# Attention with q and k resident in 64-key by 57-query tiles, filter rows turned on VectorE, and the FFT moved behind attention, in a fused conv and attention kernel

One core of one Trainium2 chip. The metric is device time of one execution, in microseconds, of the slowest (here: only) core. Executions of the kernel before on one chip agree within 1.6%. A run that lies more than 1.5% above the fastest of its kernel in the same comparison is labelled slow and is left out of all ratios.

## The reference

Two branches over one input `x` of 2048 rows by 640 columns, mixed by a gate:

```python
g = sigmoid((x * gate_w).sum(-1, keepdims=True))
# branch A: short conv on k (4 taps), times v, long conv by FFT (length 4096), times q (= x)
kv = shift_conv(k, shift_k) * v
y  = irfft(rfft(kv, 4096) * rfft(ssm_k, 4096))[:2048] + kv * ssm_D
a  = x * y
# branch B: 32 heads of 20, each query sees 8 keys at distances 0, 2, ..., 14
q, k, v = split(x @ wqkv)
b = softmax(q . k[pos - 2*off] * scale) v  @ wo
out = g * a + (1 - g) * b
```

All tensors are bfloat16. Even and odd rows never meet in branch B, so the rows are worked as two sequences of 1024.

## The kernel before

First, k's rows with their three predecessors are loaded for the conv; the predecessors go to 127 partitions:

```python
nc.sync.dma_start(kh[1:128, 0:3, :], raw(k2, 13 * D, [[16 * D, 127], [D, 3], [1, D]]))
```

Second, the gate is stored by rows of 128 partitions, and read back much later, in the middle of attention (POOL issues both):

```python
nc.gpsimd.dma_start(g_scr.rearrange("(c p two) -> p two c", p=128, two=2)[:, par, :], g_sb[...])
...
if s == 8:
    gate_loads()
```

Third, q and k are projected on PE, copied to a staging tile and moved by DMA, head by head, to partitions 32h: 20 rows of each head (these copies are called fragments below) and 11 rows that make the mask (called constants). They live in rings of three tiles, so most of the projection runs inside attention:

```python
dst = (qsets if which == 0 else ksets)[(h // 4) % 3]
frag = (dst[r:r + fb - fa, 0:w], stg[fa - f0:fb - f0, 0:w])
...
if 6 <= s < 36:
    advance(qk, 1)          # projection step inside attention
```

Fourth, attention works on 128 keys by 121 queries: six or eight score products of 121 columns, one exponential, and as many products with the values for each half (a half is two of the four heads of a tile, over one group of key blocks). The output projection is interleaved with the FFT. Fifth, in the last stage four products come straight off PSUM on DVE, and the table `T` is loaded only when the inverse FFT has left its memory.

The softmax here doesn't subtract the row's maximum and nothing guards it: scores larger than these inputs give would overflow.

Of the kernel before, what the change touches and what calls it, by code (L numbers as in the profile page):

```python
# [20 lines left out]
H = 32  # L21
# [4 lines left out]
BP = 121  # L26
NB = 17
PRE = 7
HS = 1024 + PRE
XW = 2072  # L30
NF = 11
NT = 8
KW = 128 * NB
QW = BP * NB
GROUPS = [[0, 1, 2, 3], [4, 5, 6, 7], [8, 9, 10], [11, 12, 13], [14, 15, 16]]
# [39 lines left out]
def attn_consts():  # L75
    B, C = 256.0, 512.0
    kk = np.arange(128); qq = np.arange(BP)
    kc = kk // 8 - 8; ko = kk % 8; qc = qq // 8 - 8; qo = qq % 8
    sk = np.where(kc % 2 == 0, 1.0, -1.0); sq = np.where(qc % 2 == 0, 1.0, -1.0)
    mk = np.zeros((NF, 128)); mq = np.zeros((NF, BP))  # L80
    mk[0] = kc * kc; mk[1] = kc; mk[2] = 1.0
    mq[0] = -B; mq[1] = B * (2 * qc + 1); mq[2] = -B * (qc * qc + qc) - C / 2
    for v in range(8):
        mk[3 + v] = sk * (ko == v)
        mq[3 + v] = (C / 2) * sq * np.where(v < qo, -1.0, 1.0)
    tot = np.einsum("fk,fq->kq", mk, mq)
    dlt = kk[:, None] - qq[None, :]
    inb = (dlt >= 0) & (dlt <= 7)
    assert (tot[inb] == 0).all() and (tot[~inb] <= -C / 2).all()
    for m in (mk, mq):  # L90
        assert (_np_bf16(m).astype(np.float64) == m).all()
    pos = BP * np.arange(NB)[None, :] - PRE + kk[:, None]
    valid = (((pos >= 0) & (pos < 1024)) | ((pos >= HS) & (pos < HS + 1024))).astype(np.float32)
    return dict(mk=_np_bf16(np.tile(mk, (1, NB))), mq=_np_bf16(np.tile(mq, (1, NB))),
                valid=_np_bf16(valid), ident=_np_bf16(np.eye(128)))


def ccol(sb):
    return PRE + 128 * sb + (PRE if sb >= 8 else 0)


def pos_rows(x2, p0, n):
    out = []
    for par in range(2):
        a, b = max(p0, HS * par), min(p0 + n, HS * par + S // 2)
        if a < b:
            v = x2.rearrange("(e two) d -> two e d", two=2)
            out.append((a - p0, b - a, v[par, a - HS * par:b - HS * par, :]))
    return out
# [31 lines left out]
def kernel(  # L141
# [31 lines left out]
    xS = p0.tile([128, 16, D], BF, name="xS", tag="A")  # L173
    vn = p0.tile([128, 16, D], BF, name="vn", tag="Hslot")
    Dz = p0.tile([128, 160], BF, name="Dz")
    F1b = p0.tile([128, 128], BF, name="F1b")
    M = p0.tile([128, 2, 128], BF, name="M")
    g_sb = p0.tile([128, 16], F32, name="g_sb")
    g_nat = p0.tile([128, 16], F32, name="g_nat")
    omg = p0.tile([128, NB], F32, name="omg")  # L180
    oTs = []
    for e in range(3):
        oTb = p0.tile([128, NDT, 128], BF, name=f"oT{e}")
        oTs.append(oTb)
# [3 lines left out]
    VWs = [p0.tile([128, NB, H // 2, 21], BF, name="VWa", tag="VWa"), pA.tile([128, NB, H // 2, 21], BF, name="VWb")]  # L188
    valid = pA.tile([128, NB], BF, name="valid")
    ksets, qsets, ETs = [], [], []  # L190
    for e in range(3):
        kb = pA.tile([128, KW], BF, name=f"kb{e}")
        qb = pA.tile([128, QW], BF, name=f"qb{e}")
        ksets.append(kb); qsets.append(qb)
    NET = 6
    for e in range(NET):
        ETb = pA.tile([128, 2, 512], BF, name=f"ET{e}")
        ETs.append(ETb)
    sB = ExitStack()
    p1 = sB.enter_context(tc.tile_pool(name="pB", bufs=1, side="right", reuse_waits="tile"))  # L200
# [4 lines left out]
    wg = pC.tile([128, NDT], BF, name="wg")  # L205
    wl = pC.tile([128, 4, D], BF, name="wl")


    W3 = B_wqkv.rearrange("(t p) (w n) -> p t w n", p=128, w=3)
    xq4 = x2.rearrange("(t p two) d -> p two t d", p=128, two=2)  # L210
    khs = [None] * 4

    def load_x(c):
        nc.sync.dma_start(xS[:, 4 * c:4 * c + 4, :], xq4[:, c // 2, 4 * (c % 2):4 * (c % 2) + 4, :])
# [4 lines left out]
    def load_kv(c):  # L219
        kh = p1.tile([128, 7, D], BF, name="kh", tag="kh", bufs=2)  # L220
        khs[c] = kh
        t0 = 4 * c
        eng = nc.sync if c < 2 else nc.gpsimd
# [3 lines left out]
        eng.dma_start(kh[:, 3:7, :], raw(k2, t0 * D, [[16 * D, 128], [D, 4], [1, D]]))  # L227
        eng.dma_start(vn[:, t0:t0 + 4, :], raw(v2, t0 * D, [[16 * D, 128], [D, 4], [1, D]]))

    nc.sync.dma_start(ident[:], ca["ident"].ap())  # L230
    for c0, c1 in ((0, PRE), (HS, HS + PRE), (2 * HS, XW)):
        nc.gpsimd.memset(xT[:, :, c0:c1], 0.0)
    load_x(0); load_w(2); load_x(1)
    wraw = p1.tile([128, D, 4], BF, name="wraw", tag="stg", bufs=2)
# [3 lines left out]
    load_kv(0)  # L238
    load_x(2); load_x(3)
    load_w(0); load_w(1)  # L240
    load_kv(1)
    nc.gpsimd.memset(Dz[:], 0.0)
    nc.gpsimd.memset(omg[:], 0.0)
    for e in range(NET):
        nc.gpsimd.memset(ETs[e][:], 0.0)
    for e in range(3):
        nc.gpsimd.memset(oTs[e][:], 0.0)
    for e in range(2):
        nc.gpsimd.tensor_copy(VWs[e][:, :, :, DH], valid[:].unsqueeze(2).to_broadcast([128, NB, H // 2]))

    def load_feats(e):
        for h4 in range(4):
            nc.sync.dma_start(ksets[e][32 * h4 + DH:32 * h4 + DH + NF, :], ca["mk"].ap())
            nc.sync.dma_start(qsets[e][32 * h4 + DH:32 * h4 + DH + NF, :], ca["mq"].ap())

    load_feats(0)
    for q in range(4):
        nc.gpsimd.dma_start(Dz[32 * q:32 * q + 1, :], A_ssm_D[160 * q:160 * q + 160].unsqueeze(0))
# [6 lines left out]
    def kv_gen():  # L265
        nc.vector.tensor_copy(wl[:], wraw[:].rearrange("p c j -> p j c"))
        pr = p0.tile([128, 4, 4 * D], BF, name="pr", tag="Kslot")
        yield
        for c in range(4):
            kh = khs[c]  # L270
            if c:
                nc.vector.tensor_copy(kh[:, 0:3, :], khs[c - 1][:, 4:7, :])
            for j in (0, 1, 3, 2):
                nc.vector.tensor_tensor(pr[:, j].rearrange("p (n c) -> p n c", n=4), kh[:, 3 - j:7 - j, :],  # L274
                                        wl[:, j, :].unsqueeze(1).to_broadcast([128, 4, D]), ALU.mult)
                yield
            nc.vector.tensor_tensor(pr[:, 0:2], pr[:, 0:2], pr[:, 2:4], ALU.add)
            yield
# [3 lines left out]
                                    vn[:, 4 * c:4 * c + 4, :].rearrange("p n (u i) -> p n u i", u=8), ALU.mult)  # L282
            nc.gpsimd.dma_start(raw(kvs, 4 * c * 80, [[16 * 80, 128], [S * 80, 8], [1, 320]]),
                                pr[:, 2].rearrange("p (u m) -> p u m", u=8))
            if c < 2:
                load_kv(c + 2)
            yield

    kvg = kv_gen()

# [4 lines left out]
    def transposes(c):  # L295
        for d0 in (0, 2, 4):
            nd = min(2, NDT - d0)
            tr = ppv.tile([128, 2, 4, 128], BF, name="trx", tag="trx")
            for dd in range(nd):
                for k in range(4):  # L300
                    nc.tensor.transpose(tr[:, dd, k, :], xS[:, 4 * c + k, 128 * (d0 + dd):128 * (d0 + dd) + 128], ident[:, :])  # L301
            ld.copy(xT[:, d0:d0 + nd, ccol(4 * c):ccol(4 * c) + 512],
                    tr[:, 0:nd].rearrange("p d k c -> p d (k c)"), 512 * nd, eng="a")

    def vproj(b):
        ps = ppv.tile([128, 1024], F32, name="psv", tag="psv")
        for n0, n1 in ((0, 512), (512, 640)):
            for dt in range(NDT):
                nc.tensor.matmul(ps[:, n0:n1], lhsT=xT[:, dt, BP * b:BP * b + 128], rhs=W[:, dt, 2, n0:n1],  # L309
                                 start=(dt == 0), stop=(dt == NDT - 1))  # L310
        for e in range(2):
            nc.scalar.copy(VWs[e][:, b, :, 0:DH], ps[:, 320 * e:320 * e + 320].rearrange("p (h d) -> p h d", h=H // 2))

    def gate():
        gps = ppv.tile([128, 16], F32, name="gps", tag="trx")
        for sb in range(16):
            for dt in range(NDT):
                nc.tensor.matmul(gps[:, sb:sb + 1], lhsT=xT[:, dt, ccol(sb):ccol(sb) + 128], rhs=wg[:, dt:dt + 1],
                                 start=(dt == 0), stop=(dt == NDT - 1))
        nc.scalar.activation(g_sb[:], gps[:], ACT.Exp, scale=-1.0)  # L320
        nc.vector.tensor_scalar(g_sb[:], g_sb[:], 1.0, None, ALU.add)
        nc.vector.reciprocal(g_sb[:], g_sb[:])
        for par in range(2):
            nc.gpsimd.dma_start(g_scr.rearrange("(c p two) -> p two c", p=128, two=2)[:, par, :],
                                g_sb[:, 8 * par:8 * par + 8])

    def gate_loads():
        gs = g_scr[:]
        nc.gpsimd.dma_start(omg[0:BP, 0:8], raw(gs, 0, [[2, BP], [2 * BP, 8]]))
        nc.gpsimd.dma_start(omg[0:56, 8:9], raw(gs, 2 * 968, [[2, 56], [1, 1]]))  # L330
        nc.gpsimd.dma_start(omg[63:BP, 8:9], raw(gs, 1, [[2, 58], [1, 1]]))
        nc.gpsimd.dma_start(omg[0:BP, 9:16], raw(gs, 2 * 58 + 1, [[2, BP], [2 * BP, 7]]))
        nc.gpsimd.dma_start(omg[0:119, 16:17], raw(gs, 2 * 905 + 1, [[2, 119], [1, 1]]))
        for g in range(4):
            nc.gpsimd.dma_start(g_nat[32 * g:32 * g + 32, :], raw(gs, 16 * g, [[64, 32], [1, 16]]))

# [378 lines left out]
```

## Time and profile before

| | before |
|---|---|
| median of 2 runs | 352.71 us (352.31 to 353.11) |
| PE, DVE, ACT busy | 72%, 60%, 47% of the span |
| attention starts, ends | 86 us, 212 us |
| FFT with output projection ends | 320 us |
| last stage | 34 us, 10 of them empty |

No engine is full, so the time is a sum of stages. The prediction shows the lines that carry this: engine use by stage, three waits, and the data rate in the front.

### The profile page before, as it was taken

The numbers are of one execution on the slowest core, as the hardware profiler recorded it, in microseconds if no ns is written. First come the engines' busy times: TensorE is split into PE (matmuls) and PEld (weight loads), VectorE is DVE, ScalarE is ACT, GpSimd is POOL, SyncE is SP. The second block draws the span as 40 slices with busy tenths as digits, with TensorE's granted clock in tenths as the row PEclk, the third lists the DMA queues.
The fourth block names the chain that finished last, engine by engine and source line by source line (L and its number), as shares of the span: only waits on it lengthen the run. The fifth ranks groups of instructions, "written<-read, shape, count | busy, mean of one in ns | idle before, by whom it ended". The sixth has DMA issues, their size and how long they took to land. (4 is left out here: it accounts for less than half of the span.)

```text
span 354.1 us, 9846 instructions
## 1 busy us (share of the span) xinstructions
PE 254.6 (72%) x4355; PEld 174.0 (49%) x4355; DVE 211.4 (60%) x295; ACT 165.9 (47%) x239; POOL 41.2 (12%) x67
## 2 busy tenths in 40 slices
PE   2760599958779999857877888898989488660430
PEld 2330355524336655545655655575657477660320
DVE  1400999692836565857776633844574668671595
ACT  3250264525526555634545585756565577531000
POOL 8910023010150000000000000112111000000000
PEclk9995599999659999755555556999999968867555
DMA  7375854974441499761891019217121507999165
GB/s 200 137 241 178 267 151 118 211 199 102 103 84 31 88 168 163 193 191 30 181 213 51 4 27 217 65 41 170 39 54 38 138 4 164 213 213 212 57 149 132
DMA packets 34603, 46.37 MB, mean 131 GB/s; under 512 B 23757, under 2 KB 28572, under 8 KB 33152
## 3 DMA queue, kind: packets, MB, share of 16 engines
q1 hardware_dynamic: 31088, 35.77, 42.9%
q0 software_dynamic: 2896, 8.66, 9.3%
q10 hardware_dynamic: 576, 1.31, 1.6%
q8 instruction: 34, 0.56, 0.7%
q14 instruction: 9, 0.07, 0.1%
HBM read 27.19 MB, written 7.87 MB: 99 GB/s over the span
## 5 line engine op out<-in xcount | busy, mean ns | idle before, releaser
L421 ACT ACTIVATE ET<-sc 128x726 bf16<-128x726 f32 (+1 forms) x80 | 67.1, 858 | 57.8 <-PE sc L418 57.2
L352 PE MATMUL pj<-xT,W 128*128 128x484 bf16 (+3 forms) x250 | 55.9, 368 | 6.2 <-ACT stg L128 4.0
L274 DVE TENSOR_TENSOR pr<-kh,wl 128x2560 bf16<-128x2560 bf16 x16 | 23.0, 1487 | 28.2 <-DMA kh<-in_A_k_dram 23.4
L485 PE MATMUL s<-Am,G 64*128 64x64 bf16 x1280 | 29.2, 206 | 13.9 <-DVE Hs L130 4.1
L352 PEld LDWEIGHTS <-W 128*128 128x128 bf16 x250 | 21.7, 102 | 29.8 <-issue 11.9
L418 PE MATMUL sc<-qb,kb 31*128 31x121 bf16 x544 | 36.0, 260 | 0.6 <-issue 0.6
L485 PEld LDWEIGHTS <-G 64*128 64x128 bf16 x1280 | 26.1, 105 | 17.9 <-issue 12.1
L435 PEld LDWEIGHTS <-ET 128*128 128x128 bf16 x544 | 22.4, 102 | 20.8 <-ACT ET L421 9.3
L618 PE MATMUL op<-wo,oT 128*128 128x128 bf16 (+1 forms) x170 | 27.3, 310 | 4.3 <-ACT oT L128 3.5
L130 DVE CAST stg<-pj 128x484 bf16<-128x484 f32 (+3 forms) x30 | 17.9, 598 | 20.8 <-PE pj L352 16.2
L130 DVE CAST Am<-s 128x512 bf16<-128x512 f32 x36 | 23.4, 686 | 11.5 <-PE s L468 9.9
L309 PE MATMUL psv<-W,xT 128*128 128x128 bf16 (+1 forms) x170 | 27.6, 327 | 2.8 <-DMA W<-in_B_wqkv_dram 2.8
L525 PE MATMUL i<-M,Hw 128*128 128x128 bf16 x160 | 25.6, 253 | 4.9 <-DVE Hw L513 2.6
L525 PE MATMUL i<-M,Hs 128*128 128x128 bf16 x160 | 26.0, 253 | 4.1 <-DVE Hs L512 4.1
L626 POOL DMA_DIRECT2D b_scr<-fin x18 | 9.6, 531 | 161.7 <-DVE fin L624 137.9
L128 ACT CAST Am<-s 128x512 bf16<-128x512 f32 x44 | 23.6, 610 | 6.7 <-PE s L468 4.6
L525 PEld LDWEIGHTS <-Hs 128*128 128x128 bf16 x160 | 22.5, 154 | 7.0 <-DVE Hs L512 4.5
L130 DVE CAST Hs<-s 128x1024 bf16<-128x1024 f32 x15 | 18.4, 1224 | 11.7 <-PE s L485 11.7
L301 PE MATMUL trx<-ident,xS 128*128 128x128 bf16 x80 | 7.9, 265 | 22.6 <-DMA xS<-in_A_q_dram 20.4
L525 PEld LDWEIGHTS <-Hw 128*128 128x128 bf16 x160 | 22.4, 155 | 3.0 <-DVE Hw L513 3.0
L128 ACT CAST Cm<-i 128x1024 bf16<-128x1024 f32 x15 | 15.2, 1012 | 15.9 <-PE i L525 15.7
L309 PEld LDWEIGHTS <-xT 128*128 128x128 bf16 x170 | 14.7, 106 | 15.4 <-issue 7.2
(73 smaller groups left out, 362.5 us busy)
## 6 DMA issues: line engine op xcount, KB each, us to landing
Hw<-Hs SPq DMA_DIRECT2D x10, 512.0 KB
xS<-in_A_q_dram SPq DMA_DIRECT2D x4, 640.0 KB
kv_scr<-pr POOLq DMA_DIRECT2D x4, 640.0 KB, 5.4
h_lin<-in_A_ssm_k_dram SPq DMA_DIRECT2D x8, 320.0 KB
kv<-kv_scr SPq DMA_DIRECT2D x4, 640.0 KB
qg<-in_A_q_dram SPq DMA_DIRECT2D x4, 640.0 KB
bl<-b_scr SPq DMA_DIRECT2D x4, 640.0 KB
W<-in_B_wqkv_dram SPq DMA_DIRECT2D x3, 800.0 KB
```

What stands on the lines that cost most here:

```text
L128: self.nc.scalar.copy(dst, src)
L130: self.nc.vector.tensor_copy(dst, src)
L274: nc.vector.tensor_tensor(pr[:, j].rearrange("p (n c) -> p n c", n=4), kh[:, 3 - j:7 - j, :], wl[:, j, :].unsqueeze(1).to_broadcast([128, ...
L309: nc.tensor.matmul(ps[:, n0:n1], lhsT=xT[:, dt, BP * b:BP * b + 128], rhs=W[:, dt, 2, n0:n1], start=(dt == 0), stop=(dt == NDT - 1))
L352: nc.tensor.matmul(ps[:, 0:n], lhsT=W[:, dt, which, 128 * ft:128 * ft + 128], rhs=rhs, start=(dt == 0), stop=(dt == NDT - 1))
L418: nc.tensor.matmul(sc[:, hh, BP * bb:BP * bb + BP], lhsT=kb[r:r + DH + NF, 128 * b:128 * b + 128], rhs=qb[r:r + DH + NF, BP * b:BP * b + B ...
L421: nc.scalar.activation(ETs[s % NET][:, :, 0:nw], sc[:, :, 0:nw], ACT.Exp, scale=SCALE)
L435: nc.tensor.matmul(O[:, sl * 21:sl * 21 + 21], lhsT=ET[:, hh, BP * bb:BP * bb + 128], rhs=VWs[t // 4][:, b, 4 * (t % 4) + 2 * hf + hh, :], ...
L485: nc.tensor.matmul(o, lhsT=st["G"][rows, j, r, :], rhs=Am[rows, 2 * j + r, :, :], start=(r == 0), stop=(r == 1), tile_position=(64 * c, 0) ...
L525: nc.tensor.matmul(o, lhsT=src[:, c, :, :, 8 * oc + il].rearrange("p q j -> p (q j)"), rhs=M[:, k, :], start=(k == 0), stop=(k == 1), skip ...
L618: nc.tensor.matmul(opf[:, n0:n1], lhsT=oT[:, ft, :], rhs=wo[:, ft, n0:n1], start=(ft == 0), stop=(ft == NDT - 1))
L626: nc.gpsimd.dma_start(dst, fin[r0:r0 + n, :])
```

## The change

Its intent: keep all of q and k in SBUF in 64 by 57 tiles, so that attention has no projection in it and four small products lie side by side in the array (`tile_position`); take the filter's rows apart with 32x32 transposes on VectorE; and let all FFT work follow attention, so that the output projection fills attention instead. Attention then runs in three thirds, of six of the 18 key blocks and 16 halves each. The diff has 936 lines; its core:

```diff
-    xS[128, 8, D]                      # x by 128 rows, 4 loads
+    xS[128, 18, D]                     # 18 overlapping tiles of 2 x 64 rows, tag K0
+    kvw[128, 27, D]                    # all of k and two rounds of v, tag K1
+    kq0 tag K0, kq1 tag K1             # resident q and k: heads 0-15, heads 16-31
...
     def kv_gen():                      # conv, 4 rounds; kq1 can only be written when it has ended
         nc.vector.tensor_tensor(pr[:, 2], pr[:, 0], ..., ALU.mult)
         nc.gpsimd.dma_start(kv_scr[...], pr[:, 2])     # as before: pr has one buffer
...
     def gate():
-        nc.gpsimd.dma_start(g_scr.rearrange(...), g_sb)          # 128 rows, loads later
+        for e in range(2):                                       # 57 rows; 4-byte pieces as before
+            for sub in range(2):
+                nc.gpsimd.dma_start(raw(gs, ..., [[2, QB], [4 * QB, n], [1, 1]]), gat[...])
+            nc.gpsimd.dma_start(...)
+        for g in range(4):
+            nc.gpsimd.dma_start(g_nat[32 * g:32 * g + 32, :], ...)   # at once
...
+    for k in range(25):                # all q/k projection before attention
+        advance(qk, 1); advance(kvg, 1)
...
+    for q in range(4): nc.sync.dma_start(kv[...], ...)           # 2.6 MB
+    nc.sync.dma_start(G[:], ...)                                 # 2 MB
+    nc.vector.transpose(hT[...], hns[g][...])                    # 20 times, inside attention
+    # attention: 48 halves of 24 + 24 small products, one 684-column exponential each,
+    # one step of the output projection of the third before in each half
...
+    run("aaaa", a=s1_gen(("h", 0), 0))
+    qg loads, T load                   # 3.6 MB, ahead of the first swap of halves
+    run("abababab", a=h_s2(0), b=s1_gen(("u", 0), 0))
...
+    for q in range(4): nc.scalar.copy(yt[...], ps[:, q, ...])    # last stage: ACT leaves PSUM
+    nc.vector.tensor_tensor(reg, yt, reg, ALU.mult)
```

## The prediction

> **What bounds the kernel now.** I read the page's slices first (engine use and granted clock over the span), then one table of engine use by stage, then the order of time inside each stage, then the DMA view of the first 42 us. No engine is full over the span (PE 72%, DVE 60%, ACT 47%), so the time is a sum of stages, each with its own limit. Columns of the table: stretch, its length, then busy us and instruction count of PE, weight load, DVE, ACT, POOL, then granted clock, DMA share, GB/s.
>
> ```profile
> 11.00:86.00 75.00, 53.93 (x412) 30.35 (x414) 43.87 (x31) 29.35 (x63) 14.67 (x20) 0.86 0.64 176
> 86.00:143.00 57.00, 51.39 (x643) 29.67 (x643) 32.91 (x66) 30.97 (x38) 6.84 (x10) 0.88 0.58 104
> 143.00:212.00 69.00, 52.90 (x1085) 39.03 (x1085) 45.23 (x84) 36.60 (x44) 0.00 (x0) 0.52 0.45 111
> 212.00:276.00 64.00, 56.58 (x927) 39.49 (x924) 35.99 (x48) 38.48 (x56) 9.55 (x18) 0.95 0.38 92
> 276.00:320.00 44.00, 30.10 (x768) 28.30 (x767) 31.12 (x39) 26.73 (x36) 0.00 (x0) 0.81 0.68 149
> 320.00:330.00 10.00, 0.06 (x16) 0.06 (x16) 0.09 (x1) 0.06 (x1) 0.00 (x0) 0.68 0.75 184
> 330.00:354.00 24.00, 7.22 (x512) 4.94 (x512) 18.60 (x30) 0.00 (x0) 0.00 (x0) 0.50 0.45 112
> ```
>
> Front (to 86), attention with 30 of the 50 q/k projection chunks (to 143), attention with the filter FFT of three groups (to 212), FFT with output projection (to 276), FFT alone (to 320), ten empty us, the last stage. The third row matters most: the clock is halved for 69 us although PE is busy for 53 of them.
>
> Two waits explain the empty places. In the front, x arrives late; the single-engine DMA below is the reason. Near the end everything stands for T.
>
> ```profile
> PEld L301 <- DMA xS<-in_A_q_dram: 20.6, 2, 15.1
> DVE pr L274 <- DMA kh<-in_A_k_dram: 23.4, 2, 23.2
> PE i L673 <- DMA T<-cf_T: 10.9, 1, 10.9
> ```
>
> Data rate in 40 slices of the stretch from 10 to 16 us:
>
> ```profile
> GB/s 401 401 410 384 393 401 375 375 350 273 239 137 102 77 51 26 26 26 26 26 26 26 26 26 26 26 26 26 26 26 51 0 51 26 26 26 26 26 26 26
> ```
>
> The rate falls from 400 to 26 GB/s: one engine works, on the load of k's first three rows (127 partitions, 476 KB). 487 KB at 26 GB/s is some 19 to 22 us,[...] kh came at 35.8, the third piece of x at 39.05.
>
> [...]
>
> **The change part by part.**
>
> *Front.* x is now gathered as 18 overlapping tiles, and 13 of them are queued ahead of the 127-partition load, which stays. Work for those 13 on PE is some 1.7 us each[...], from 11 us as before: to about 32. Before, the slow load ran 9.4 to 31.7; the x tiles ahead of it add some 125 KB on its engine, so it ends near 38, kh lands at 42, the last five x tiles at 47. PE waits from 32 to 47, and ends values and gate at 61. Then all 50 q/k chunks run at once[...].
>
> That is not what ends the front. q and k now live in two whole tiles; the second reuses the memory of k and v of the conv. Its constants are queued on SP ahead of the third block's fragments, so SP stands until DVE has done the conv: starting at 42, four rounds of 13.5 us (before: 35.8 to 76.4 for three) end at 96. Constants then take some 7 us and the fragments of that block some 10 (174 KB each; before 85 KB took 0.71 us to issue, or 120 GB/s). The staging tile is double, so the fifth block waits until 114, and its last tiles run cold. Attention begins at 121 (before: 86). Here is the price of keeping q and k resident: 35 us later, against 30 chunks (150 matmuls of some 0.2 us, 31 us) taken out of attention.
>
> *Attention.* 80 exponentials become 48. From 726 columns 778 ns and 968 columns 977 ns, one of 684 is 743 ns: ACT falls from 67.1 to 35.7 us, and it isn't the limit. PE at the halved clock before: the eight scores of one half took 0.54 us, eight values products 0.32[...].
>
> ```profile
> 204.31 0.39 PE L435 MATMUL O<-VWb,ET 128*128 128x21 bf16 x8
> 204.63 0.59 PE L418 MATMUL sc<-qb,kb 31*128 31x121 bf16 x8
> 205.48 0.39 PE L435 MATMUL O<-VWb,ET 128*128 128x21 bf16 x8 [0.27 <-ACT ET L421]
> ```
>
> After: 24 and 24 smaller matmuls for each half, four side by side. The only 16-tile stage here (last stage, 32x32 tiles) made 93 in 1.25 us, 13.4 ns for load and matmul. If issue sets that, 48 x 13.4 + 0.2 = 0.85 us[...]. I take 1.15. First third (16 halves): 18.5 us. In the others the output projection of the third before is mixed in, on average 1.2 us cold or 0.6 warm: 32 x 2.45 = 78 us cold, 32 x 1.5 = 48 warm. Before, with 5 projection matmuls of about 1.0 us in 1.55 us the clock was full; with FFT matmuls of 0.97 in 2.36 it stayed halved. The new mix is 40 to 53%, so I give cold 70%: 70 us. Then the last six projections alone: 13.[...] Attention and projection end at 121 + 18.5 + 70 + 13 = 222 (attention alone ended at 212 before).
>
> *FFT.* Now all five filter groups stand here and no projection. Vector work for a group: 16 copies of 512 columns (0.60 ACT, 0.69 DVE), 12 of 1024 (1.01, 1.23), four products of 1.22: shared out, 14 us. PE at full clock: 64 first-stage matmuls 1.8, 256 second-stage 4.4, 64 inverse 4.1, 10.3 us, and 18 at the halved. So it is vector-bound by a little when warm. With hand-overs 15.5 a group; start 17, three groups with scaling of qg 49, last 24: 90 us (before 108). End 312.
>
> *Last stage.* T is loaded early: the empty ten us go. Before, a round is four products off PSUM and one sum, 3.43 us on DVE. Now four copies on ACT (0.58 each, 2.3) beside two DVE operations of 1.16: 2.32. With 6.1 us of scaling bl (16 x 0.38) in front: about 5 + 12.6 + 4 for the last stores = 22 (before 34).
>
> Sum: 121 + 101 + 90 + 22 = 334; I say 333.
>
> **The rivals.** (1) Small tiles pay[...]. Attention is 60 us in place of 88, total some 305. For it: i2's 13.4 ns; against it: 69 us of halved clock before. (2) [...]everything stays cold: 1.5 us a half, attention 24 + 89, FFT partly cold at 105: total some 370. (3) SP isn't held up as I say, because the conv starts sooner or the last blocks overlap: attention at 105, total 317. The wait for kh of 23.2 us speaks against it. (4) Saturated DMA at the end of the front[...] runs into attention and costs 10 more.
>
> **Range and chances.** The parts are uncertain by about 15 (attention), 8 (FFT), 6 (front), 4 (rest): together 18.5, so 24 either way for 8 in 10. 2% faster is 345.7, 0.7 of that deviation away: faster 0.76, same 0.16, slower 0.08.
>
> **What would show it.** A front with a PE gap near 32 to 47 and another near 104 to 114, SP waiting for DVE's last conv product; attention starting near 121; cold clock in it, at 1.15 us a half first and 2.4 later; ACT's exponentials near 36 us in all; FFT near 90 us with ACT and DVE above 75% and PE below; no wait for T. Wrong if the exponentials queue on ACT, if the clock is full through attention, or if attention starts before 110.

The sum is 121 + 101 + 90 + 22 = 334 us, given as 333. In the 121, the column rate of PE behind the 1.7 us of a tile of x and behind the q/k projection (45 us, 9.1 for each of five blocks) is cut; in the 101, the dearer case of 1.5 us a half is cut, so that 1.15 stands as my estimate between 0.85 and 1.5, and the 0.2 us in 0.85 is an allowance that no trace shows. DVE's transposes: taken as hidden and so in no term. The output projection's 0.6 us a half warm and 1.2 cold are estimates; a block of it took 1.64 us in e_op_burst (214.05 to 215.69, warm), so six blocks in 16 halves are 0.62. Cold means the halved clock (granted 0.50), warm the full one (1.00).

What the trace of the kernel before shows for these steps: from 116.19 to 117.22 us five products of 484 columns at granted clock 1.00, 2.35 columns per ns (an estimate from that figure: 1.36 us for ten of 320 columns, 46 us for 25 x 4356); a DMA share of 0.06 of the 16 engines, so one of them, at 26 GB/s from 12.5 to 14.4 us; and a clock of 1.00 from 116 to 121 and 0.50 from 170.9 to 179, the two mixes that the prediction compares. The 125 KB on that engine are an estimate too, a 16th of some 2 MB, from the rates of 400 and 26 GB/s.

## The result, and the profile after

The changed kernel takes 413.18 us (413.04 to 413.32, 2 runs): 1.1715 of before, interval 1.1655 to 1.1774. It is slower by 17%. A ratio is the mean time of one kernel's fast runs over that of the other's in the same rounds, so not quite the quotient of the medians. Later runs were on other chips, where before takes 355 to 357 us, so I compare ratios; 0.01 of ratio is 3.5 us. The changed kernel itself was timed in two runs only and never beside its variants. A step from it to a variant therefore compares ratios from two chips, and that a chip scales both kernels alike is assumed, not shown.

Engine use of the changed kernel by stage, columns as in the prediction's first table: front to the gate, q/k projection, projection and waiting, first third of attention, the other two, tail of the projection, FFT, last stage.

```profile
11.00:64.00 53.00, 35.07 (x351) 26.19 (x351) 18.83 (x13) 24.37 (x52) 9.02 (x10) 0.84 0.65 189
64.00:90.00 26.00, 25.84 (x131) 12.83 (x131) 11.94 (x9) 10.75 (x21) 8.93 (x8) 0.93 0.85 124
90.00:167.00 77.00, 29.68 (x117) 13.84 (x118) 17.43 (x11) 13.57 (x28) 4.48 (x9) 0.67 0.56 101
167.00:200.00 33.00, 16.38 (x764) 13.80 (x763) 15.58 (x36) 13.09 (x19) 0.26 (x4) 0.55 0.76 193
200.00:272.00 72.00, 66.62 (x1700) 43.85 (x1700) 40.77 (x99) 29.98 (x43) 0.57 (x3) 0.57 0.16 52
272.00:287.00 15.00, 11.52 (x121) 8.23 (x120) 5.71 (x10) 4.15 (x6) 0.00 (x0) 1.00 0.16 51
287.00:387.00 100.00, 70.46 (x1904) 64.74 (x1904) 69.01 (x81) 64.28 (x94) 0.00 (x0) 0.78 0.53 121
387.00:410.00 23.00, 7.28 (x532) 5.83 (x529) 17.03 (x28) 12.44 (x26) 5.96 (x12) 0.68 0.43 117
```

The third row is the catastrophe: 77 us in which PE works 30, DVE 17, ACT 14. Against the prediction's own stages:

| | before | predicted | after | after less predicted |
|---|---|---|---|---|
| conv ends | | 96 | 128.6 | +33 |
| attention starts | 86 | 121 | 167.5 | +46.5 |
| attention and projection take | | 101 | 119.5 | +18.5 |
| FFT takes | 108 | 90 | 100 | +10 |
| last stage takes | 34 | 22 | 23.5 | +1.5 |

The front is over half of the miss. Waits of the changed kernel (engine, line, what it waited for: us in all, times, longest):

```profile
ACT stg L119 <- DMA kq<-stg: 62.7, 3, 38.2
PE pj L340 <- ACT stg L119: 47.2, 3, 33.1
DVE pr L248 <- DMA kv_scr<-pr: 37.0, 3, 20.9
DVE pr L248 <- DMA kvw<-in_A_k_dram: 31.7, 1, 31.7
...
POOL g_nat L318 <- DMA g_scr<-gat: 26.8, 1, 26.8
PE trx L283 <- DMA xS<-in_A_q_dram: 23.2, 2, 16.2
...
DVE Hs L416 <- DMA Hw<-Hs: 6.0, 1, 6.0
```

Read from below: x arrives late (the load on one engine, as predicted), POOL stands for the gate's stores, the conv stands 37 us for its own stores, then the projection stands because its staging tile is not emptied. POOL's timeline (start, duration, engine, what; in brackets the idle time before it and its releaser) shows how the gate comes into the conv's way:

```profile
70.12 0.91 POOL L260 DMA_DIRECT2D kv_scr<-pr  x1 [12.45 <-DVE pr L256]
...
106.41 2.04 POOL L318 DMA_DIRECT2D g_nat<-g_scr  x4 [26.75 <-DMA g_scr<-gat]
115.94 0.20 POOL L319 TENSOR_SCALAR omg<-g_nat 128x16 f32<-128x16 f32 x1 [7.48 <-DMA g_nat<-g_scr]
116.91 0.97 POOL L260 DMA_DIRECT2D kv_scr<-pr  x1 [0.77 <-issue]
```

The third round of the conv was done at 96, and its store went out at 116.9, since POOL works in order and stood for 8 KB of gate. The fourth round's last tap product (j = 2) overwrites that buffer, so DVE stood 20.9 us. The kernel before has the same reuse of `pr`, where it cost DVE 4.8 us in all; here it is 37.0. The six gate stores took some 26 us to land; before, the two stores of 128 rows had taken 5.7 (medians). Then SP, which waits for the conv's end before it may write the second half of q and k:

```profile
128.63 1.49 SPq L328 DMA_DIRECT2D kq<-ca_feat  x4
130.22 43.94 SPq L355 DMA_DIRECT2D kq<-stg  x22
```

22 fragments take 44 us to be queued. Lastly PE in the first third of attention:

```profile
191.07 0.48 PE L496 MATMUL sc<-kq 31*64 31x57 bf16 x18 [5.58 <-issue]
...
200.01 0.34 PE L521 MATMUL O<-VW,ET 64*64 64x21 bf16 x10 [5.96 <-issue]
```

Two stalls of together 11.5 us, "issue", so nothing that the profile shows; the DMA was full at that time (1.01 of 16 engines from 184 to 200).

### The profile page after: what moved, and what is told of

Its sections match the earlier page's. It is cut to its first block, busy times and chain, and to the rows that moved or that the text cites. A ratio compares the mean times of both kernels' runs of the same rounds, so it can differ in the third digit from the quotient of the medians.

```text
span 410.6 us, 12313 instructions
## 1 busy us (share of the span) xinstructions
PE 264.1 (64%) x5611; PEld 190.4 (46%) x5616; DVE 196.3 (48%) x285; ACT 175.2 (43%) x292; POOL 35.7 (9%) x58
## 4 chain that ended last, share of the span: by engine, by line
DMA 27%; PE 26%; DVE 19%; issue 15%; POOL 5%; ACT 5%; SPq 1%; POOLq 0%; DVEq 0%; ACTq 0%
DMA kq<-stg 8%; DMA g_scr<-gat 6%; PE i L428 6%; PE op L553 6%; DMA Hw<-Hs 5%; PE O L521 3%; PE sc L496 3%; PE s L396 3%; DMA kv_scr<-pr 3%; DVE oS L531 2%; DVE hT L472 2%; DVE Hw L417 2%; DMA g_nat<-g_scr 2%; DMA b_scr<-fin 2%; PE tr L539 2%
## 5 line engine op out<-in xcount | busy, mean ns | idle before, releaser
L340 PE MATMUL pj<-xT,W 128*128 128x456 bf16 (+3 forms) x245 | 56.1, 395 | 47.5 <-ACT stg L119 47.2
L119 ACT CAST stg<-pj 128x512 bf16<-128x512 f32 (+3 forms) x50 | 24.9, 537 | 78.8 <-DMA kq<-stg 62.7
L499 ACT ACTIVATE ET<-sc 128x684 bf16<-128x684 f32 x48 | 35.4, 742 | 49.8 <-PE sc L496 48.5
L248 DVE TENSOR_TENSOR pr<-kvw,wl 128x2560 bf16<-128x2560 bf16 x16 | 23.1, 1483 | 68.8 <-DMA kv_scr<-pr 37.0
L472 DVE STREAM_TRANSPOSE hT<-hn 128x512 bf16<-128x512 bf16 x20 | 20.3, 1031 | 39.1 <-PE pj L340 39.1
L553 PE MATMUL op<-wo,oT 128*128 128x320 bf16 x120 | 32.9, 432 | 2.8 <-DVE fin L558 2.6
L290 PE MATMUL psv<-W,xT 128*128 128x320 bf16 x180 | 30.3, 321 | 4.5 <-DMA W<-in_B_wqkv_dram 4.5
L521 PE MATMUL O<-VW,ET 64*64 64x21 bf16 x1152 | 25.0, 203 | 8.9 <-issue 6.0
L496 PE MATMUL sc<-kq 31*64 31x57 bf16 x1152 | 25.0, 228 | 7.8 <-issue 6.1
L521 PEld LDWEIGHTS <-ET 64*64 64x64 bf16 x1152 | 19.6, 142 | 12.7 <-issue 6.6
L283 PE MATMUL trx<-ident,xS 128*128 128x128 bf16 x90 | 9.2, 244 | 23.2 <-DMA xS<-in_A_q_dram 23.2
L290 PEld LDWEIGHTS <-xT 128*128 128x128 bf16 x180 | 18.2, 105 | 11.6 <-issue 4.1
## 6 DMA issues: line engine op xcount, KB each, us to landing
kv_scr<-pr POOLq DMA_DIRECT2D x4, 640.0 KB, 12.3
```

Source lines behind the costliest of these rows:

```text
L119: self.nc.scalar.copy(dst, src)
L248: nc.vector.tensor_tensor(pr[:, j].rearrange("p (n c) -> p n c", n=4), kh[:, 4 * c + 3 - j:4 * c + 7 - j, :], wl[:, j, :].unsqueeze(1).to_ ...
L290: nc.tensor.matmul(ps[:, 0:320], lhsT=xT[:, dt, 128 * m:128 * m + 128], rhs=W[:, dt, 2, n0:n0 + 320], start=(dt == 0), stop=(dt == NDT - 1))
L340: nc.tensor.matmul(ps[:, 0:nb * wd], lhsT=W[:, dt, which, 128 * ft:128 * ft + 128], rhs=rhs, start=(dt == 0), stop=(dt == NDT - 1))
L472: nc.vector.transpose(hT[:, g].rearrange("p (c n) i -> p n c i", c=2)[:, 16 * p:16 * p + 16], hns[g][:].rearrange("p (a n) -> p n a", n=64 ...
L496: nc.tensor.matmul(sc[64 * sub:64 * sub + 64, hh, QB * mb:QB * mb + QB], lhsT=kqt[r:r + DH + NF, t % 4, si, 0:KB], rhs=kqt[r:r + DH + NF, ...
```

## The experiments

My theory after reading: (1) the gate's trip and the reuse of `pr` delay the conv, (2) the load on one engine adds to it, (3) constants and fragments queue in order behind the conv, (4) the bulk loads of kv and G stall PE, (5) the loads of qg and T delay the FFT's first swap. The rival for the front: DMA has so many bytes to move before attention that order hardly matters. Edits are shown against the changed kernel unless stated.

| run | ratio to before | 95% interval | attention starts |
|---|---|---|---|
| after | 1.1715 | 1.1655 to 1.1774 | 167.5 |
| e_gate_late | 1.1311 | 1.1192 to 1.1430 | 160.9 |
| e_gate_attn | 1 fast run in 4; median 399.87 beside 355.59 | none | 156.4 |
| e_k_split | 1.1122 | 1.0994 to 1.1249 | 152.2 |
| e_pr_two | 1.1331 | 1.1250 to 1.1413 | 150.4 |
| s1_front | 1.0903 | 1.0843 to 1.0963 | 142.7 |
| s2_front_queues | 1.0811 | 1.0724 to 1.0898 | 142.7 |
| s4_feats_last | 1.0784 | 1.0680 to 1.0888 | 119.2 |
| e_op_burst | 1.1798 | 1.1708 to 1.1888 | 167.2 |
| e_bulk_spread | 1.1581 | 1.1483 to 1.1678 | 167.8 |
| e_bulk_paced | 1.1479 | 1.1377 to 1.1581 | 166.9 |
| e_bulk_stores | 1.1325 | 1.1205 to 1.1445 | 165.8 |
| e_swap_first | 1.1567 | 1.1491 to 1.1643 | 165.6 |
| s3_all | 1.0811 | 1.0726 to 1.0896 | 137.4 |
| s5_all | 1.0655 | 1.0584 to 1.0726 | 119.3 |
| b_k_split | 0.9510 | 0.9393 to 0.9626 | 68.2 |
| b_best | 0.9711 | 0.9649 to 0.9773 | 69.4 |
| b_best2 | 0.9450 | 0.9396 to 0.9503 | 68.5 |

The profiled runs of e_k_split, e_gate_attn, s2_front_queues, s4_feats_last and e_bulk_stores were slow (up to 2.9% above the fastest of their kernel). I take from them when things start and which waits are there, and the size of an effect from the fast runs' ratios. The FFT shows how far the traces scatter: in the changed kernel and the eleven variants whose edits leave it alone it takes 96.8 to 101.3 us, the changed kernel's being the longest. So an effect of a few us is not told from scatter by one trace. All runs but e_port_spread were correct; that one was run once (387.51 us, state unknown), so it has no ratio.

### The front: gate, load, buffer

**e_gate_late**: the gate's DMA chain moved behind the conv's last store.

```diff
     gate()
     ...
         if k == 8:
             load_h(0); load_h(1)
+    gate_dma()          # the stores, loads and omg that stood in gate()
```

> The same kernel, but the gate's trip through DRAM (six stores of four-byte pieces, four loads) is issued on POOL after the conv's last store, not before the conv's third store. Theory A (POOL takes its work in order, so the conv's third store stands behind the gate's 27 us wait, and the conv's end behind that store): the third store goes out near 97 us in place of 116.9, the wait of DVE's pr for kv_scr of 20.9 us goes, the conv ends near 108 to 112, attention starts near 148 to 152 in place of 167.5, and the time is 393 to 400 us (13 to 20 less than 413). Theory B (the DMA is full in this stretch and order matters little): the third store is issued early but lands late, the wait stays at 12 us or more, and the time moves by less than 5 us.

Measured: the conv's last store went out at 116.0, not 128.9, but the wait of DVE for the stores was still 23.0 us, and attention started only 6.6 us sooner. The gate's stores now took 32 us and lay beside the fragments. Half right: POOL's order cost the conv some 13 us; the wait for the store did not go, so it has a second cause. The ratio fell by 0.040, which is 14 us and more than attention's start gained; about 4 of the rest lie in the FFT (97.5 us in place of 101.3), which the edit does not touch.

**e_gate_attn**: the same chain at the 24th half of attention.

```diff
+        if i == 24:
+            gate_dma()
```

> The kernel after with one edit: the gate's trip through DRAM is issued in the middle of attention (half 24). The one-engine load stays. This separates the prediction's step 'conv ends at 96' from the load. Theory A (POOL's order and the crowding by the gate's stores made the conv late): the conv's last product ends at 98 to 108 in place of 128.6, attention starts at 138 to 148 in place of 167.5, ratio to before 1.09 to 1.12. Theory B (the one-engine load is the main cause, and the gain of s1_front was mostly the load's): attention starts after 155, ratio above 1.135.

Measured: conv's last product from 116.4, attention at 156.4, 11 us sooner. That lies at theory B's edge: the gate is a part, not the main part. POOL stood 8.5 us for the gate stores issued here, which landed within 9.6 us (27.5 in the changed kernel's front). DVE still stood 2.2, 13.8 and 9.6 us for stores of kv.

**e_k_split**: no load on one engine.

```diff
-            nc.sync.dma_start(kh[1:128, 0:3, :], raw(k2, 13 * D, [[16 * D, 127], ...
+            nc.sync.dma_start(kh[1:113, 0:3, :], raw(k2, 13 * D, [[16 * D, 112], ...
+            nc.sync.dma_start(kh[113:128, 0:3, :], raw(k2, (13 + 16 * 112) * D, [[16 * D, 15], ...
```

> The same kernel, but k's first three rows on 127 partitions are loaded as 112 and 15 partitions. Theory A (the load on one engine is what makes x and k late): the 16.2 us gap of PE before the last x tiles shrinks to under 5 us, the conv starts near 30 in place of 44.3, and all that follows moves by 10 to 14 us, attention to near 155, the time to 400 us. Theory B (what follows is set by the gate's trip and the stores on POOL, which shift less, or by full DMA): the gap in the front goes but attention starts at most 4 us sooner and the time stays above 408.

Measured: the gap of PE before the last x tiles fell from 16.2 to 1.8 us, the conv started at 29.5 (44.3), attention at 152.2, 15 us sooner; ratio 0.059 lower, 21 us (in plain time, on another chip, 17 us). Theory A, and more than it hoped for.

**s1_front**: e_k_split and e_gate_attn together.

> Two edits on one kernel: k's first rows loaded as 112 and 15 partitions, and the gate's trip through DRAM issued in the middle of attention (half 24), where DMA is 15% busy. Theory A (three things add up: the one-engine load, POOL's order, and gate stores that crowd the DMA in the front; moved only behind the conv they gave 6.6 us at attention's start because they then crowded the fragments): conv starts at 30, waits for kv_scr stay under 5 us in all, the conv ends at 86 to 92, attention starts at 125 to 135, ratio to before 1.05 to 1.08. Theory B (the fragments themselves[...] are the limit): the conv ends early but attention still starts after 145, ratio above 1.09.

Measured: attention at 142.7, 25 us sooner: 15 + 11, so the two add up. But the conv ended at 104, not 86 to 92: DVE stood 23.5 us for its stores of kv even with the gate gone. Between the two theories, and it points at the buffer.

**e_pr_two**: the conv's last product in a tile of its own with two buffers, nothing else changed.

```diff
-            nc.vector.tensor_tensor(pr[:, 2]..., pr[:, 0]..., vns[c % 2]..., ALU.mult)
+            kvo = pC.tile([128, 4 * D], BF, name="kvo", tag="kvo", bufs=2)
+            nc.vector.tensor_tensor(kvo[:]..., pr[:, 0]..., vns[c % 2]..., ALU.mult)
```

> The kernel after with one edit: the conv's last product goes to a tile of its own with two buffers, not to the slot of pr that the next round's last product writes. Theory A (the step of the prediction that failed is 'four rounds of 13.5 us': a round also stands until the store of the round before has landed, 37 us in all in after): the conv's last product ends at 96 to 104 in place of 127, as the prediction had it, with the one-engine load and the gate's trip as they are; attention starts at 135 to 148, ratio to before 1.08 to 1.11. Theory B (the waits for the stores only hide DMA that has to be done before attention anyway): the conv ends near 100 but attention starts after 155, ratio above 1.13.

DVE's timeline, its last conv product:

```profile
96.14 1.49 DVE L257 TENSOR_TENSOR kvo<-pr,kvw 128x2560 bf16<-128x2560 bf16 x1 [5.81 <-DMA kvw<-in_A_v_dram]
```

The conv ends at 97.6, where the prediction had it (96), with the late load and the gate's trip left as they were. So the term that the prediction missed is the wait for the store of the round before. That the end agrees so closely with 96 is partly luck: the conv started 3 us later than predicted and stood 5.8 us for v, while the rounds' own work was shorter than the 13.5 us that the prediction took (see below). Yet attention starts at 150.4: of 31 us, 17 arrive. SP's timeline says why:

```profile
89.87 16.61 SPq L356 DMA_DIRECT2D kq<-stg  x7
110.86 3.21 SPq L329 DMA_DIRECT2D kq<-ca_feat  x4
115.41 41.64 SPq L356 DMA_DIRECT2D kq<-stg  x22
```

SP is still at the fragments of the blocks before until 106, and the 22 fragments again take 42 us. From the conv's end to attention it is now 53 us, 39 in the changed kernel; the prediction had 25. So behind the conv waits a second limit, the way of constants and fragments. Behind the first scores, moreover, ACT stood 12.3 us for a fragment (1.1 in the changed kernel), so most of the 17 us were lost again, and the ratio of 1.1331 is in theory B's range: the buffer sets the conv's end, and the way behind it holds attention.

### The front: constants and fragments

**s2_front_queues**: on s1_front, constants and fragments for partitions from 64 up on POOL's queue.

```diff
-            nc.sync.dma_start(kq[t // 4][o:o + r1 - r0, ...], stg[...])
+            (nc.sync, nc.gpsimd)[h4 // 2].dma_start(kq[t // 4][o:o + r1 - r0, ...], stg[...])
```

> As s1_front, but the constants and fragments that go to partitions from 64 up are issued on POOL's queue, those below on SP's. Theory A[...]: the 22 fragments after the conv take 22 to 28 us in place of 44, attention starts 12 to 18 us sooner than in s1_front, and so the ratio falls by 0.035 to 0.05 against it. Theory B (the 16 engines are shared, full, or the fragments wait for the staging tiles only): less than 4 us.

Measured: attention at 142.7 in both; the ratios' intervals overlap. Theory A had the two queues work side by side; it is not borne out. DMA was 96% busy from 106 to 114 at only 131 GB/s. But the run is no clean test of two queues: POOL stood 11.7 us for its store of kv and 5.0 us for its constants, its fragments landed some 30 us after their issue, and SP still took 42 us for its half of them. What two free queues would do is not shown.

**s4_feats_last**: on s1_front, the second block of constants behind all fragments.

```diff
-            if ft == 2:
-                feats(1)
...
+            if ft == NDT - 1:
+                feats(1)
```

> As s1_front (k's rows split, gate's trip in the middle of attention), with the second block of constants (1.5 MB) queued on SP after the last fragments, not ahead of the third block's. Theory A (SP's order: the constants take 18 us of the way from the conv's end to attention, and the first eight halves don't read them): the way from the conv's last store to the first scores falls from 38.6 us to 20 to 26, attention starts at 124 to 131, and the time falls by 12 to 18 us against s1_front (ratio to before 1.04 to 1.06, s1_front's being 1.0903). Theory B ([...]PE then waits for the constants at the ninth half): attention starts sooner but stops for 10 us or more near its eighth half, and the time falls by 5 us or less.

Measured: attention starts at 119.2, 23 us sooner than in s1_front, and gives nearly all of it back. PE's timeline:

```profile
138.07 0.22 PE L505 MATMUL sc<-kq 31*64 31x57 bf16 x1 [6.21 <-DMA kq<-ca_feat]
142.71 0.53 PE L505 MATMUL sc<-kq 31*64 31x57 bf16 x23 [4.42 <-DMA kq<-ca_feat]
147.84 0.25 PE L505 MATMUL sc<-kq 31*64 31x57 bf16 x1 [4.16 <-DMA kq<-ca_feat]
152.28 0.53 PE L505 MATMUL sc<-kq 31*64 31x57 bf16 x23 [4.19 <-DMA kq<-ca_feat]
```

Each of the four pieces (374 KB) lands some 4.7 us after the one before, 80 GB/s, and PE stands for each: 19 us. The DMA was full meanwhile (0.96 to 1.08 of its engines from 135 to 155), with wo and kv beside the pieces, so 80 GB/s is not the pace of a piece alone. The interval of the ratio overlaps s1_front's. Theory B: at this point bytes count, not order.

**e_port_spread**: on s4_feats_last, those constants, as zeros, to every eleventh partition. Its output is wrong, which doesn't matter for the time.

```diff
-            r = slice(32 * h4 + DH, 32 * h4 + DH + NF)
+            r = slice(32*h4+DH, 32*h4+DH+NF) if e == 0 else slice(h4, h4 + 11 * NF, NF)
```

> As s4_feats_last, but the second block of constants goes to 44 partitions spread evenly (every eleventh) in place of 44 that lie in four runs of eleven; its values are zeros and the scores of those tiles don't read the mask rows, so the result is wrong on purpose, with the same bytes in the same shape at the same place in the queue. Theory A[...]: PE's waits for the constants at the ninth and later halves (19 us in s4_feats_last) shrink to under 6 us. Theory B (the source, one DRAM tensor read four times, or the order of the queue behind kv and G sets the pace): the waits stay at 12 us or more, summed over those for the constants or for later data.

What the run tests is whether the partitions that a copy goes to set its pace. PE's timeline of this run:

```profile
145.36 0.54 PE L506 MATMUL sc<-kq 20*64 20x57 bf16 x24 [14.87 <-DMA kq<-ca_featz]
```

The wait is 14.9 us in place of 19.0, and 15.6 us pass from the first issue to the last landing, 97 GB/s, while wo and kv move beside it (26.5 us in s4_feats_last, where fragments still lay ahead). My expectation of under 6 us was missed. The same bytes went at 97 GB/s in place of 80, but with other loads beside them in both runs, so a part of the gain may be theirs. That the partitions set the pace is not shown. What holds these copies to 80 to 135 GB/s stays open.

### Attention

**e_op_burst**: the output projection of a third in one piece at its end.

```diff
-                opg = op_gen(g2)
...
-        if opg is not None:
-            advance(opg, 2 if i % 8 == 7 else 1)
+                op_burst(g2)        # six transposes and projections, as after the last third
```

> The same kernel, but the output projection of each third is done in one piece when the third is complete, as the last one is done already, not one step for each half of attention. Theory A (the mixed-in projection runs at the halved clock[...]): each burst of six runs warm in 13 us, the thirds in between at 0.905 us a half in 15 to 16 us, so attention with all projections takes 100 to 106 us in place of 119.5 and the time is 396 to 401. Theory B (the burst waits for its one PSUM tile, the copies and the 57-row stores and is itself cold): a burst takes 20 us or more and the time stays within 5 us of 413.

Measured: no gain (420.14 us, intervals overlap). A burst ran warm (clock 0.86 from 207 to 222) and took 15.4 us, but the sixteen halves between two bursts took 24 us (220 to 244), not 15: without the projection to fill the time PE stands for DVE's normalization, up to 2.5 us at a time, beside the transposes. DVE is busy 20.2 of the 23 us from 222 to 245, and PE 15.6. The cold clock is real (0.50 in the changed kernel from 200 to 262, 0.59 here from 222 to 255), but in this run a half waits for DVE. In the changed kernel PE is busy 66.6 of those 72 us, so two limits lie close together. Neither theory holds as it stands: the burst was shorter than theory B had it, and the time 7 us longer.

**e_bulk_spread**: kv and G in twelve pieces on SP, one every third half.

> The same kernel as after, but the loads of kv and G (4.6 MB) are not queued in one go before attention; they are cut into twelve pieces, one every third half from the eighth on. Theory A (the two stalls of PE of 5.6 and 6.0 us, which the trace puts to nothing that it shows, come from a full DMA): they go, the first sixteen halves take 20 to 22 us in place of 32, and the time is 10 to 12 us less than after's (ratio to before 1.137 to 1.143, after's being 1.1715). Theory B (they are part of the start of attention, or DVE's transposes set the pace there): the stalls stay or become waits on DVE, and the ratio falls by less than 0.012.

This run did not do what its edit says: nothing made SP wait, so it issued the four pieces of kv from 181 to 185 us. Stalls of 6.8 and 7.9 us stayed. It decides nothing. In program order is not the same as in step.

**e_bulk_paced**: 24 pieces, one issued by ACT behind each exponential of halves 3 to 26.

```diff
+            nc.scalar.dma_start(kv[32*q:32*q+32, c, 32*b:32*b+32, :], ...)   # or 1/8 of G
```

> The same kernel as after, but kv and G are loaded in 24 pieces of 160 and 256 KB, one issued by ACT behind each exponential of halves 3 to 26, so that they can't run ahead (in e_bulk_spread SP issued the pieces within 5 us, since nothing held it: that run didn't test what it should). Theory A (PE's two stalls of 5.6 and 6.0 us come from a full DMA): DMA stays under 70% in each stretch of attention, no PE gap there is over 2 us, the first sixteen halves take 20 to 22 us in place of 32, and the ratio to before falls by 0.028 to 0.034 from after's 1.1715. Theory B (the stalls come from something else in the start of attention): they stay, and the ratio falls by less than 0.012.

Measured: no "issue" gap above 2 us was left, but ACT stood 8.1 us, which the profile puts to the load of a filter tile, before it issued a piece, and PE stood 7.1 us for ACT. Ratio 0.024 lower: between the theories, spoilt by a stall of its own.

**e_bulk_stores**: twelve pieces on SP, each behind the store of one projection block, which waits for DVE.

```diff
         if hf == 1:
             op_store(j)
+            bulk(j)
```

> The kernel after with one edit: kv and G are loaded in twelve pieces, each queued on SP behind the store of one output projection block, so SP can't run ahead and ACT issues nothing. (In e_bulk_paced one stall of 7 us stayed, on ACT, which waited there before issuing a piece: its own artefact.) Theory A (a full DMA at the start of attention stalls PE): no PE gap of over 2 us between 170 and 205, the first projection matmul comes 9 to 12 us sooner than after's 203.1, and the ratio falls from 1.1715 to 1.137 to 1.148. Theory B (the stall moves to the place where the pieces now run, or the wait moves to the FFT): ratio above 1.155.

Engine use of this kernel from 184 to 200, columns as above:

```profile
184.00:192.00 8.00, 6.19 (x247) 4.91 (x248) 3.56 (x12) 4.37 (x7) 0.38 (x2) 0.50 0.39 95
192.00:200.00 8.00, 7.87 (x212) 5.16 (x211) 4.96 (x12) 3.41 (x6) 0.00 (x0) 0.57 0.11 30
```

and of the changed kernel:

```profile
184.00:192.00 8.00, 2.42 (x126) 2.07 (x125) 1.56 (x5) 1.48 (x3) 0.00 (x0) 0.50 1.01 212
192.00:200.00 8.00, 1.91 (x86) 1.56 (x87) 1.18 (x4) 1.87 (x3) 0.00 (x0) 0.50 1.01 302
```

PE works 14.1 of 16 us in place of 4.3, with DMA at 0.39 and 0.11 in place of 1.01. No gap of 2 us is left in attention, the first projection matmul comes 25.9 us after the first scores in place of 35.6, and the ratio falls by 0.039. Two of the four runs were fast, and 1.1325 lies a little past theory A's range. Theory A: bulk loads that nothing needed for another 85 us stalled PE. The kept traces say more of what PE stood for where the profile says "issue". They list a DMA queue of kind "instruction" (q8; in the changed kernel 44 packets of 16 KB, beside 11,227 matmuls and weight loads). In the changed kernel its packets started at 179.6, 188.1 and 197.5 us, here at 182.4, 186.4, 190.1 and 194.2. The two stalls end 1.6 and 1.5 us after the packets of 188.1 and 197.5 landed, the two such gaps of the changed kernel's FFT 1.4 and 1.6 us after those of 304.7 and 312.5, and all 74 "issue" gaps of PE over 2 us in the kept traces end 1.3 to 1.8 us after such a packet landed. From this I infer that PE stood for instructions that came late; what a packet holds is not in the traces. Why a packet starts late is not in the traces; full DMA fits.

### The FFT

**e_swap_first**

```diff
-    qg loads; T load
     run("abababab", a=h_s2(0), b=s1_gen(("u", 0), 0))
+    qg loads; T load
```

> The same kernel, but the loads of qg and T (3.6 MB) are queued on SP after the first swap of filter halves, not before it. Theory A (the first swap stands behind them): DVE's 5.95 us wait for Hw goes and the time falls by 5 to 8 us, to 405 to 408. Theory B: the loads then delay the second group's swap by the same, and the time moves by less than 2 us.

Measured: the 6.0 us wait for Hw is gone, ratio 0.015 lower. But the time itself hardly moved (412.28 us, where 405 to 408 was expected; the trace is 1.4 us shorter), and the wait is also only 0.0 to 1.7 us long in eleven variants that keep the loads ahead of the swap; 6 us stand only in the changed kernel and in e_bulk_stores. So what the edit gains is not shown, and theory A stays open.

### Together, and back on the kernel before

**s3_all**: s2_front_queues with e_bulk_spread and e_swap_first.

> As s2_front_queues, with kv and G loaded in twelve pieces through attention and the first swap queued ahead of qg and T. Both theories expect some 15 us less than s2_front_queues if the pieces are independent (10 to 12 and 5); with all of theory A the time is 335 to 350 on a chip where before takes 353, ratio 0.95 to 0.99. If the stalls in the start of attention only change their cause, the gain against s2_front_queues is 5 us or less.

Measured: the same 1.0811 as s2_front_queues, far from 0.95 to 0.99. PE now had stalls of 3.2, 9.8 and 3.8 us in attention: SP's pieces ran ahead again, and what the front gave (attention at 137.4) went there.

**s5_all**: s4_feats_last with e_bulk_paced and e_swap_first.

> As s4_feats_last, with the paced loads of kv and G and the first swap ahead of qg and T. If theory A holds in both, the parts add up: 350 to 358 us on a chip where before takes 356, ratio 0.985 to 1.01, attention starts near 127, FFT near 237. If only one holds, ratio 1.02 to 1.05.

Measured: 378.68 us, 1.0655. Attention started at 119.3, but PE stood 12.0, 4.8, 4.9 and 2.6 us for the constants, so the ratio is outside both ranges. The best of the changed kernel's variants, and still 6.5% slower than before.

**b_k_split**: the kernel before with the split load, nothing else.

> The kernel before, with k's first three rows loaded as 112 and 15 partitions and nothing else. Theory A (the one-engine load held up both kernels: PE's 15.1 us wait for x and DVE's 23.2 us wait for kh are its work): attention starts 8 to 12 us sooner and the ratio is 0.965 to 0.98. Theory B (before, the next limit in the front comes at once, the third piece of x or the values' copies): ratio above 0.985.

Measured: 338.95 us, 0.951. Attention starts at 68.2 in place of 86.0, DVE's wait for kh falls from 23.2 to 4.1 us at the longest. More than theory A had. The wait for T stayed (12.2 us).

**b_best**: b_k_split with T in its own memory at the start of the FFT, and the changed kernel's last stage.

```diff
+    T = p3.tile([128, 64, 2, 32], BF, name="T")          # loaded at the start of the FFT
...
-            nc.vector.tensor_tensor(rq, yv, rq, ALU.mult)            # off PSUM, four times
+            nc.scalar.copy(yt[...], ps[:, q, ...])                   # four times
+        nc.vector.tensor_tensor(reg, yt[:, 0:m, :], reg, ALU.mult)
```

> The kernel before with three edits: k's rows split (alone 0.951), T loaded into its own memory at the start of the FFT, and the last stage as the change has it (four copies off PSUM on ACT, one product and one sum on DVE). Theory A (the parts are independent: the wait for T was 10.9 us, and the last stage's rounds fall from 3.43 to 2.3 us each): 17 + 10 + 5 us less than before, ratio 0.905 to 0.925, 322 to 329 us where before takes 355. Theory B (with T early the wait for the last product of the inverse FFT or for the blend takes its place): ratio 0.935 to 0.951.

Measured: 344.64 us, 0.971, slower than b_k_split, worse than both theories. ACT's timeline in its last stage:

```profile
320.49 0.85 ACTq L684 DMA_DIRECT2D out_dram<-qg  x2
321.44 1.95 ACT L680 CAST yt<-i 128x480 bf16<-128x480 f32 x4 [3.36 <-DVE qg L682]
325.80 0.85 ACTq L684 DMA_DIRECT2D out_dram<-qg  x2
```

In the kernel before ACT issues half of the output's stores; it stood for DVE's sum before each, and the next round's copies came after: 5.3 us a round. The changed kernel issues them on POOL.

**b_best2**: the same with these stores on POOL.

> As b_best, with the output's stores issued by SP and POOL in place of SP and ACT. Theory A (in b_best ACT, in order, stood until DVE's sum before it issued its two stores of 0.85 us, and the next round's copies came after: rounds of 5.3 us in place of 2.3): the rounds fall to 2.2 to 2.8 us, the last stage from 34 us (b_best: inverse FFT's end near 307 to 342.5) to 20 to 24, ratio 0.92 to 0.94, 327 to 334 us. Theory B (the T load or the copies cost what the rest gains): ratio 0.95 or more.

Measured: 337.01 us, 0.945, theory B by a hair. ACT no longer stands, but the first inverse matmul starts at 304.8 in place of 311.8, so T was worth 7 us there, and the stage then takes 29.5 us in place of 24.1. PE is busy 6.7 us of it; it stands 2.1 to 2.8 us four times in "issue" gaps like those of e_bulk_stores, and DVE waits 4.7 us at the longest for ACT's copies. The gain over the split alone (0.951) is inside the intervals. Both beat the kernel before by some 5%.

## Why the prediction was wrong

By its own steps:

- **Front, conv ends at 96: failed.** This is the step "four rounds of 13.5 us (before: 35.8 to 76.4 for three) end at 96". Each round also stands until its predecessor's store has landed: 37.0 us in all. From 44.3, four rounds of 11.6 us of own work and these 37 give 128. I looked at DVE's durations and not at who reads `pr`; in the kernel before that wait was 4.8 us and showed in no line that I read. Part of it is inside my 13.5 us, 1.2 us a round, beside a copy of 0.65 us that the change takes out. e_pr_two removes the wait alone and puts the end at 97.6; the match with 96 is partly luck, as said there. A part of the wait was the gate's trip, which the prediction did not mention at all (11 us of attention's start, e_gate_attn).
- **From the conv's end to attention, 25 us: failed.** "Constants then take some 7 us and the fragments of that block some 10." The constants took 18 to 20 at some 80 GB/s, the 22 fragments 44 to queue; the way took 39 us. I had read 120 GB/s off a copy of 85 KB that takes 0.71 us to issue. That time says nothing of the rate: a fragment of 170 KB in the changed kernel also takes 0.71 us to issue. The prediction's rival (4), DMA full at the end of the front, named it and gave it 10 us. The two failed steps are 33 + 14 of the 47 us.
- **The load on one engine: right as a mechanism and as placed** (26 GB/s at a DMA share of 0.06 in the kernel before; split in e_k_split, PE's gap fell from 16.2 to 1.8 us; PE gap 34 to 50 predicted 32 to 47; conv's start 44.3, predicted 42). It cost the changed kernel some 21 us by ratio (17 in plain time) and the kernel before some 17, so it explains the time and not the difference.
- **Attention, first third 18.5 us: failed.** It took 32.5. The small products were cheaper than I took them, 0.905 us a half and not 1.15, but PE stood 11.5 us in two stalls, each of which ended 1.5 to 1.6 us after a packet of the instruction queue landed, under bulk loads that I had not placed in time at all (e_bulk_stores: 9.7 us sooner, ratio 0.039 lower). Also the transposes took 1.03 us each; the prediction had taken them shorter, by an estimate that rested on no trace:

```profile
L499 ACT ACTIVATE ET<-sc 128x684 bf16<-128x684 f32 x48 | 35.4, 742 | 49.8 <-PE sc L496 48.5
...
L472 DVE STREAM_TRANSPOSE hT<-hn 128x512 bf16<-128x512 bf16 x20 | 20.3, 1031 | 39.1 <-PE pj L340 39.1
```

- **Exponentials 35.7 us in all: right** (35.4). **The rest of attention 70 us, mostly cold: right** (72 at clock 0.57), in part by luck: the 70 is a mix of 78 and 48, and the halves' own products were 8 us cheaper in these 32 halves than the 1.15 in it, so something else ran dearer. That the cold clock sets it was argued and isn't shown: e_op_burst warmed the projection and gained nothing.
- **FFT 90 us: too short by 10.** The failed step is "vector-bound by a little when warm", with ACT and DVE above 75%: measured were DVE 69%, ACT 64% and PE 70% at clock 0.78, so no engine is full. The trace shows the 6.0 us wait for Hw and two "issue" gaps of PE of 3.7 and 4.0 us; that e_swap_first removes any of the 10 is not shown, and groups of 17 to 19 us in place of 15.5 were not tested. The cause stays open.
- **Last stage 22 us without the wait for T: right** (23.5). On the kernel before it brought nothing that the runs can tell from zero.
- **The range** came from independent errors of 6 us in the front and 15 in attention. The front had the largest error, and it had the least: it is the stage with most queues in order, one after another. "Slower" had been given a chance of 0.08.

What stays open: what holds the copies to 11 or 20 partitions to 80 to 135 GB/s; why a packet of the instruction queue starts late when the DMA is full; what the order of qg and T costs; and whether all fixes in one kernel, e_pr_two and e_bulk_stores with s1_front, would reach before. s5_all, without these two, recovers 37 of the 60 us.

## What to carry to other kernels

Holding operands resident moves their production ahead of the stage that uses them; before counting what it takes out, add up the bytes and the in-order queues that must now finish first. For each buffer that a store reads, ask who writes it next, and for each queue, what stands behind a wait in it: 8 KB of gate in small pieces (11 us of attention's start in e_gate_attn) and one single-buffered product (37.0 us of waits) cost more here than any arithmetic. And issue a big load as late as its use allows, paced by something that really waits; a place in the program order didn't pace the queue in e_bulk_spread, where SP issued the four pieces of kv from 181 to 185 us.
